# Two instructions of each chunk's preparation, the scan on VectorE and the logarithm on ScalarE, kept at their written place among the dense steps

## The chip, the cores and the metric

The kernel runs on one core of a Trainium2 chip. The metric is the device time of one launch in microseconds (us). The core's engines each work through a queue of their own, in order: TensorE (PE; its weight loads are listed as PEld), VectorE (DVE), ScalarE (ACT), GpSimd (POOL) and SyncE (SP), which here starts nearly all transfers. An instruction waits at the head of its queue until what it reads is written and what it overwrites is no longer needed, and all that stands behind it on that engine waits too.

## What is computed

```python
# batch 4, heads 8, sequence 768, head size 48
for t in range(S):                       # attention with a decaying state
    state = alpha[:, :, t, :, None] * state + einsum('bhd,bhe->bhde', k[:, :, t], v[:, :, t])
    y[:, :, t] = einsum('bhd,bhde->bhe', q[:, :, t], state)
x = y.transpose(0, 2, 1, 3).reshape(3072, 384)
h = x @ w_in                             # 384 -> 2048
x = (maximum(h, 0) + moe_alpha * minimum(h, 0)) @ w_out          # 2048 -> 384
a, b = x @ w1, x @ w2                    # 384 -> 1024
out = (a * b @ w3) @ w_out2              # 1024 -> 1024 -> 384
```

All of it is float32.

## The kernel before

The sequence of each batch is cut into chunks of 128 positions (`CH`): 24 chunks in all (`NSTEP`), numbered n = 0 to 23, and chunk n ends a batch where n leaves 5 when divided by 6. The tokens are also cut into six tiles T of 512 (`TA`), four chunks to a tile. A matrix product of float32 accuracy is made of three products of shorter parts (high by high, high by low, low by high), so that one product of a weight block takes nine matmuls of 512 columns.

For each chunk, `prep(n)` makes from the decays a running product P (`scan`, a scan on VectorE, line 221), then on ScalarE its logarithm (`Ln`, line 235) and the exponential of minus that (`Exp`, line 236), which gives 1/P in `r`; VectorE makes q times P (`qt`, line 228), k times r (`kn`, line 237), P times r (line 238) and from both the corrected `kn` (line 239), which I call the last kn. `scores(n)` is 32 small matmuls of `kn` and `qt` (tile `scp`, recorded at line 244), masked on VectorE (`sc`, line 279). `kT(n)` turns `kn` over on TensorE. `chunk(n)` forms the update of the state (`uy`), the output of the chunk (`yp`, `uy`), and then, at its end, `scores(n + 1)`.

The dense steps of the first layer are `G1(T, f)`, nine matmuls into the tile `h` and then the chain u (ScalarE, line 419), g (VectorE, 421), high part of gs (ScalarE, 426), low part of gs (VectorE, 427); and `G2(T, f)`, nine matmuls of gs into three accumulators (lines 435, 436, 438), two steps later. When a tile is through, its three accumulators are copied out on ScalarE (tile `x1e`, line 73).

The attention of tile T is woven into the dense steps of tile T - 1: `attn_units` lists pieces of work (`chunk(n)`, `kT(n + 1)`, `prep(n + 2)`, in that order), and `attend()` hands out the next piece after every G1 and every G2, evenly over the steps. So `prep(n + 1)` is written about one dense step ahead of `chunk(n)`, whose end needs its `kn`.

What is written is not yet the order of the engines. On SyncE the order is as written. On the other engines a scheduler orders the instructions when the kernel is built: by its own estimate of times it takes, as an engine comes free, an instruction that it holds to be ready. `tc.keep_in_program_order(ins)` binds one instruction behind the one that is written ahead of it on its engine. In the kernel before, u and g of G1 are bound so from T = 2 on, the matmuls of the attention among themselves, and the scan only in the opening. The buffers of P (`albuf`) are two, that of `r` is one.

Of the kernel before, what the change touches and what calls it, by code (L numbers as in the profile page):

```python
# [15 lines left out]
AF = mybir.ActivationFunctionType  # L16
# [16 lines left out]
SPT = TA // CH  # L33
# [31 lines left out]
def fused_kernel(ctx, tc, qk, al, vv, wf, ws, m_alpha, ident, maskn, out):  # L65
    nc = tc.nc
    act, dve, pool, pe, sp = nc.scalar, nc.vector, nc.gpsimd, nc.tensor, nc.sync

    def f32(ap):
        return ap.bitcast(F32)  # L70
# [144 lines left out]
    def prep(n, last=False):  # L215
        if n >= NSTEP:
            return
        t = st.pop(("qk", n))
        P = albuf[n % 2]
        flatP = P.rearrange("p a t -> p (a t)")  # L220
        scan = dve.tensor_tensor_scan(out=flatP, data0=flatP, data1=scan1.rearrange("p a t -> p (a t)"),  # L221
                                      initial=0.0, op0=ALU.mult, op1=ALU.max)
        if last:
            tc.keep_in_program_order(scan)
        pool.memset(P[:, :, 0:1], 0.0)
        Pv = P[:, :, 1:]
        qt = ap2.tile([128, NP, CH], F32, tag="qt", name="qt")
        dve.tensor_tensor(out=qt, in0=t[:, 0], in1=Pv, op=ALU.mult)
        r = ap2.tile([128, NP, CH], F32, tag="r", name="r", bufs=1)
        kn = ap2.tile([128, NP, CH], F32, tag="kn", name="kn")  # L230
        pend = ap2.tile([128, NP, 1], F32, tag="pend", name="pend")
        pool.tensor_copy(out=pend, in_=P[:, :, CH:])
        st["pend", n], st["qt", n], st["kn", n] = pend, qt, kn

        act.activation(out=r, in_=Pv, func=AF.Ln)
        act.activation(out=r, in_=r, func=AF.Exp, scale=-1.0)
        dve.tensor_tensor(out=kn, in0=t[:, 1], in1=r, op=ALU.mult)
        dve.tensor_tensor(out=r, in0=Pv, in1=r, op=ALU.mult)
        dve.scalar_tensor_tensor(out=kn, in0=r, scalar=2.0, in1=kn, op0=ALU.subtract, op1=ALU.mult)
# [143 lines left out]
    def attn_units(T):  # L383
        w = T % 2
        n0 = T * SPT
        u = []
        if T == 2:
            u += [lambda: prep(n0), lambda: load(n0 + 2)]
        if T <= 2:
            u += [lambda: (untie(), scores(n0, w), kT(n0, w)), lambda: prep(n0 + 1)]  # L390
        for n in range(n0, n0 + SPT):
            ahead = T > 1 or n < n0 + SPT - 1
            u += [lambda n=n, ahead=ahead: (ahead and load(n + 3), chunk(n, w, ahead)),
                  lambda n=n, ahead=ahead: ahead and kT(n + 1, w)]
            if T > 1 or n < n0 + SPT - 2:
                u += [lambda n=n: prep(n + 2)]
            if n == n0 + 2:
                u += [lambda: xsplit(T, 0, 2)]
        return u
# [4 lines left out]
    def mm3(ps, pairs, first, last):  # L404
        n = len(pairs)
        for i, (w, x) in enumerate(pairs):
            pe.matmul(ps, w, x, start=first and i == 0, stop=last and i == n - 1)  # L407
# [4 lines left out]
    def G1(T, f):  # L412
        x, w = xt[T], r_in[f]
        ps = pab.tile([128, TA], F32, tag="h", name="h")
        mm3(ps, [(w[:, i, k], x[:, 0, k]) for k in range(KD) for i in range(2)]
            + [(w[:, 0, k], x[:, 1, k]) for k in range(KD)], True, True)
        sg, sa = sgn[:, f:f + 1], salpha[:, f:f + 1]
        u = gp.tile([128, TA], F32, tag="m", name="u", bufs=1)
        both = [act.activation(out=u, in_=ps, func=AF.Identity, scale=sg)]  # L419
        gt = gp.tile([128, TA], F32, tag="g", name="g")  # L420
        both += [dve.scalar_tensor_tensor(out=gt, in0=ps, scalar=sa, in1=u, op0=ALU.mult, op1=ALU.max)]  # L421
        if T > 1:
            for ins in both:
                tc.keep_in_program_order(ins)
        s = g_t[T, f] = gp.tile([128, 2, TA], F32R, tag="gs", name="gs", bufs=3)
        act.activation(out=s[:, 0], in_=gt, func=AF.Identity, scale=sg)  # L426
        dve.scalar_tensor_tensor(out=s[:, 1], in0=gt, scalar=sg, in1=f32(s[:, 0]), op0=ALU.mult, op1=ALU.subtract)  # L427
# [17 lines left out]
    with tc.manual_schedule(engines={mybir.EngineType.SP}):  # L445
# [65 lines left out]
        for g in range(NG + LAG):  # L511
            T, f = seq[g] if g < NG else (NTA, 0)
# [50 lines left out]
            if g < NG:  # L563
                G1(T, f)
                attend()
# [87 lines left out]
        for q in range(NTA * NJ):  # L653
            T, j = divmod(q, NJ)
# [19 lines left out]
    with tc.If(bad > 0):  # L674
        with tc.tile_pool(name="fa", bufs=1) as fa:
# [5 lines left out]
            with tc.For_i(0, B, 1) as b:  # L681
                dve.memset(S_, 0.0)
                with tc.For_i(0, NC_B, 1) as c:
# [7 lines left out]
                    for g in range(CH // TG):  # L691
                        yt = fa.tile([2, TG, NP, D], F32, name="yt")
                        for i in range(TG):
# [10 lines left out]
                            for hh in range(2):  # L704
                                r = slice(64 * hh, 64 * hh + 64)
# [11 lines left out]
                        for k, to, a, e, n_, g_ in whole + [piece + (KD,) for piece in PIECES]:  # L717
                            hh, pr = g_ // 2, 2 * (g_ % 2) + a
                            sp.dma_start(out=dst[:, :, :, k, to:to + n_].rearrange("b c t e -> (b c) t e"),
                                         in_=yt[hh:hh + 1, :, pr, e:e + n_])  # L720

        with tc.tile_pool(name="fb", bufs=1) as fb:
# [6 lines left out]
            for f in range(NF):  # L729
                for o, dst in enumerate((wi[:, f].rearrange("p k f -> p (k f)"), wo[:, f])):  # L730
                    t = fb.tile([128, DM, 2], I32, name="rw")
                    sp.dma_start(out=t.bitcast(I16).rearrange("p n c -> p (n c)")[:, :4 * DM - 1],
                                 in_=wf[f, :, o].bitcast(I16)[:, 1:])
# [88 lines left out]
```

## Time and profile before

| | |
|---|---|
| three runs | 844.17, 847.43, 847.84 us (median 847.43) |
| the profiled execution | 846.02 us, of which the span from first to last instruction is 844.2 us |
| PE | 824.3 us busy (98% of the span) in 5160 matmuls |
| DVE | 458.3 us busy (54%) |
| ACT | 355.3 us busy (42%) |
| POOL | 10.3 us busy (1%) |
| granted TensorE clock, mean | 0.998 of full speed |

Busy time is what an engine's instructions took; the rest of the span it waited. A matmul of 512 columns is listed with 0.39 us, but the next one starts 0.23 us after it, so the starts say how fast TensorE goes. An idle time is listed with the instruction that ended it and with what that instruction had waited for. The three figures behind each wait are the sum, the number of times, and the longest.

### The profile page before, as it was taken

What the parts mean: (1) busy time and instruction counts of PE and PEld (TensorE: products, weight loads), DVE (VectorE), ACT (ScalarE), POOL (GpSimd) and SP (SyncE); (2) the same over time, 40 slices, a digit from 0 to 9 for tenths busy, and PEclk for the clock granted to TensorE, in tenths of its full rate; (3) what the DMA queues carried; (4) which work ended last, traced back from release to release, by engine and by line L of the source; (5) the groups of instructions that cost most, each with busy time, mean ns of one, the idle gap of its engine ahead of it and who ended that gap; (6) DMA issues with size and microseconds to landing.
All of it is one profiled execution on the core that took longest, in us unless ns stands there. A gap on an engine that the chain in (4) does not pass through costs nothing.

```text
span 844.2 us, 12696 instructions
## 1 busy us (share of the span) xinstructions
PE 824.3 (98%) x5160; PEld 673.1 (80%) x5160; DVE 458.3 (54%) x643; ACT 355.3 (42%) x562; POOL 10.3 (1%) x53
## 2 busy tenths in 40 slices
PE   8989999999999999999999999999999999999996
PEld 4567888888887788878888889988888888888885
DVE  7799966774766576765345634652434425322221
ACT  4568764534544554554335634522223232222222
POOL 0000000000000000000000000000000000000000
PEclk9999999999999999999999999999999999999999
DMA  8647555330774377354104207320402203010101
GB/s 314 212 168 245 197 176 183 118 110 10 225 236 146 119 231 256 131 165 168 48 3 159 78 1 255 119 75 1 150 0 75 75 31 119 1 38 0 38 1 41
DMA packets 49106, 99.60 MB, mean 118 GB/s; under 512 B 4880, under 2 KB 25488, under 8 KB 49040
## 3 DMA queue, kind: packets, MB, share of 16 engines
q1 hardware_dynamic: 48800, 98.62, 34.6%
q8 instruction: 42, 0.69, 0.3%
q14 instruction: 24, 0.20, 0.1%
q10 hardware_dynamic: 240, 0.10, 0.0%
HBM read 75.63 MB, written 18.35 MB: 111 GB/s over the span
## 4 chain that ended last, share of the span: by engine, by line
PE 83%; DMA 2%; DVE 1%; ACT 1%; issue 0%; SPq 0%; DVEq 0%; ACTq 0%
PE ab L407 23%; PE h L407 20%; PE acc L407 12%; PE acc L435 6%; PE acc L438 6%; PE acc L436 6%; PE w L407 4%; PE uy L244 3%; DMA al<-in_al_dram 2%; PE scp L244 2%; PE yp L244 1%; PE kTp L263 1%; DVE al L221 0%; DVE y L149 0%; ACT u L419 0%
## 5 line engine op out<-in xcount | busy, mean ns | idle before, releaser
L407 PE MATMUL h<-x,w 128*128 128x512 f32 x864 | 214.3, 392 | 3.2 <-ACT w L73 1.4
L407 PE MATMUL ab<-x,w 128*128 128x512 f32 x864 | 203.6, 389 | 0.0
L407 PEld LDWEIGHTS h<-x,w 128*128 128x128 f32 x864 | 160.9, 188 | 39.8 <-DVE g L421 2.6
L407 PEld LDWEIGHTS ab<-x,w 128*128 128x128 f32 x864 | 162.1, 188 | 33.6
L435 PE MATMUL acc<-gs,w 128*128 128x512 f32 x288 | 114.7, 398 | 0.0
L614 DVE TENSOR_TENSOR c<-ab,a 128x512 f32<-128x512 f32 x48 | 33.1, 690 | 147.3 <-PE ab L407 147.3
L436 PE MATMUL acc<-gs,w 128*128 128x512 f32 x288 | 112.3, 390 | 0.0
L421 DVE SCALAR_TENSOR_TENSOR g<-h,salpha,u 128x512 f32<-128x512 f32 x96 | 71.8, 748 | 69.2 <-ACT u L419 69.1
L407 PE MATMUL acc<-cs,w 128*128 128x512 f32 x432 | 105.8, 389 | 0.0
L426 ACT ACTIVATE gs<-g,sgn 128x512 fp32r<-128x512 f32 x96 | 69.3, 722 | 75.5 <-DVE g L421 75.4
L419 ACT ACTIVATE u<-h,sgn 128x512 f32<-128x512 f32 x96 | 65.4, 681 | 82.5 <-PE h L407 82.4
L427 DVE SCALAR_TENSOR_TENSOR gs<-g,sgn,gs 128x512 fp32r<-128x512 f32 x96 | 71.9, 749 | 42.7 <-ACT gs L426 42.6
L407 PEld LDWEIGHTS acc<-cs,w 128*128 128x128 f32 x432 | 81.0, 188 | 17.2 <-DVE cs L617 0.4
L438 PE MATMUL acc<-gs,w 128*128 128x512 f32 x288 | 80.9, 389 | 0.0
L73 ACT ACTIVATE a<-ab 128x512 f32<-128x512 f32 x48 | 28.7, 597 | 111.9 <-PE ab L407 111.9
L73 ACT ACTIVATE cs<-c 128x512 fp32r<-128x512 f32 x48 | 30.2, 630 | 91.5 <-DVE c L614 91.5
L435 PEld LDWEIGHTS acc<-gs,w 128*128 128x128 f32 x288 | 54.1, 188 | 12.6 <-issue 1.2
L438 PEld LDWEIGHTS acc<-gs,w 128*128 128x128 f32 x288 | 54.1, 188 | 11.5
L436 PEld LDWEIGHTS acc<-gs,w 128*128 128x128 f32 x288 | 54.1, 188 | 10.5
L617 DVE TENSOR_TENSOR cs<-c,cs 128x512 fp32r<-128x512 f32 x48 | 33.2, 691 | 30.8 <-ACT cs L73 30.8
L142 ACT ACTIVATE top<-raw 128x768 f16<-128x768 bf16 (+1 forms) x39 | 41.8, 1071 | 16.9 <-DVE y L149 12.0
L221 DVE TENSOR_TENSOR_SCAN al<-al,scan 128x516 f32<-128x516 f32 x24 | 29.4, 1230 | 25.2 <-DMA al<-in_al_dram 25.2
(73 smaller groups left out, 673.8 us busy)
## 6 DMA issues: line engine op xcount, KB each, us to landing
raw<-in_ws_dram SPq DMA_DIRECT2D x22, 767.8 KB, 5.2
qk<-in_qk_dram SPq DMA_DIRECT2D x24, 512.0 KB, 5.9
raw<-in_wf_dram SPq DMA_DIRECT2D x16, 767.8 KB, 5.9
ws_d<-y SPq DMA_DIRECT2D x22, 384.0 KB, 2.6
al<-in_al_dram SPq DMA_DIRECT2D x24, 256.0 KB, 4.9
v<-in_vv_dram SPq DMA_DIRECT2D x24, 256.0 KB, 5.9
alx<-in_al_dram SPq DMA_DIRECT2D x8, 768.0 KB, 4.6
x_d<-x1e SPq DMA_DIRECT2D x18, 256.0 KB, 4.3
```

The source lines that it names most:

```text
L73: act.activation(out=out, in_=in_, func=AF.Copy)
L142: ins = act.activation(out=z[:, :n].bitcast(F16).rearrange("p (n c) -> p n c", c=2)[:, :, 1], in_=t.bitcast(BF16)[:, :, 2], func=AF.Copy)
L244: ins = pe.matmul(*a, **k)
L407: pe.matmul(ps, w, x, start=first and i == 0, stop=last and i == n - 1)
L419: both = [act.activation(out=u, in_=ps, func=AF.Identity, scale=sg)]
L421: both += [dve.scalar_tensor_tensor(out=gt, in0=ps, scalar=sa, in1=u, op0=ALU.mult, op1=ALU.max)]
L426: act.activation(out=s[:, 0], in_=gt, func=AF.Identity, scale=sg)
L427: dve.scalar_tensor_tensor(out=s[:, 1], in0=gt, scalar=sg, in1=f32(s[:, 0]), op0=ALU.mult, op1=ALU.subtract)
L435: pe.matmul(acc[T][m], r_out[f][:, 0, c], s[:, 0], start=f == 0, stop=False)
L436: pe.matmul(acc[T][m], r_out[f][:, 1, c], s[:, 0], start=False, stop=False)
L438: pe.matmul(acc[T][m], r_out[f][:, 0, c], s[:, 1], start=False, stop=f == NF - 1)
L617: dve.tensor_tensor(out=s[:, 1], in0=c, in1=f32(s[:, 0]), op=ALU.subtract)
```

## The change

Three bindings. The scan of `prep(n)` is kept in program order not only in the opening but also for n > 8, that is from chunk 9 on. The logarithm is kept in program order for the same chunks. And u and g of G1 are kept in program order from T = 1 on, where it was from T = 2 on. Nothing is computed otherwise, and no instruction is added or removed. (Behind line 235 the line numbers of the changed kernel are two higher.)

```diff
@@ prep(n, last=False)
         scan = dve.tensor_tensor_scan(out=flatP, data0=flatP, data1=scan1.rearrange("p a t -> p (a t)"),
                                       initial=0.0, op0=ALU.mult, op1=ALU.max)
-        if last:
+        if last or n > 2 * SPT:
             tc.keep_in_program_order(scan)
...
-        act.activation(out=r, in_=Pv, func=AF.Ln)
+        ln = act.activation(out=r, in_=Pv, func=AF.Ln)
+        if n > 2 * SPT:
+            tc.keep_in_program_order(ln)
         act.activation(out=r, in_=r, func=AF.Exp, scale=-1.0)
@@ G1(T, f)
-        if T > 1:
+        if T > 0:
             for ins in both:
                 tc.keep_in_program_order(ins)
```

How the engines' orders move is shown at three places. The first is VectorE around chunk 8, where the numbers behind a name tell the buffers apart: g_1559 and gs_1561 belong to one dense step, kn_1569 and al1_110 to chunk 9, kn_1700 and al0_109 to chunk 10, r_1828 to chunk 11. Before:

```order
L427 SCALAR_TENSOR_TENSOR gs_1506<-g_1504,sgn_78,gs_1506 128x512
L279 TENSOR_TENSOR sc_1529<-scp_1510,msk_76 128x512
L237 TENSOR_TENSOR kn_1700<-qk_1486,r_1699 128x512
L221 SCALAR_TENSOR_TENSOR al1_110<-al1_110,scan1_111 128x516
L238 TENSOR_TENSOR r_1699<-al0_109,r_1699 128x512
L239 SCALAR_TENSOR_TENSOR kn_1700<-r_1699,kn_1700 128x512
L421 SCALAR_TENSOR_TENSOR g_1559<-h_1547,salpha_79,u_1557 128x512
L427 SCALAR_TENSOR_TENSOR gs_1561<-g_1559,sgn_78,gs_1561 128x512
```

And now:

```order
L423 SCALAR_TENSOR_TENSOR g_1559<-h_1547,salpha_79,u_1557 128x512
L429 SCALAR_TENSOR_TENSOR gs_1561<-g_1559,sgn_78,gs_1561 128x512
L221 SCALAR_TENSOR_TENSOR al1_110<-al1_110,scan1_111 128x516
L228 TENSOR_TENSOR qt_1566<-qk_1011,al1_110 128x512
L239 TENSOR_TENSOR kn_1569<-qk_1011,r_1568 128x512
L304 TENSOR_TENSOR sst1_113<-sst0_112,yT_1618 128x256
L240 TENSOR_TENSOR r_1568<-al1_110,r_1568 128x512
L306 TENSOR_TENSOR sst1_113<-sst1_113,pend_1464 128x256
L241 SCALAR_TENSOR_TENSOR kn_1569<-r_1568,kn_1569 128x512
```

Before, at this place VectorE already prepares chunk 10 and scans chunk 11, and chunk 9 has long been prepared; now the scan of chunk 9 stands behind gs_1561, and its last kn closes the row. From chunk 9 on each scan stands in this way behind the gs written ahead of it.

The second place is TensorE at the same chunk: the matmuls that close `chunk(8)`, and the scores of chunk 9 (`scp`). Before:

```order
L244 MATMUL yp<-qt,sst_112 64x128
L244 MATMUL scp<-qt,kn 64x128 x16
L407 MATMUL h<-x,w_86 128x512 x9
L263 MATMUL kTp<-idn,kn 128x128 x4
L435 MATMUL acc_1429<-gs,w_84 128x512
L436 MATMUL acc_1429<-gs,w_84 128x512
```

And now:

```order
L246 MATMUL yp<-qt,sst_112 64x128
L409 MATMUL h<-x,w_86 128x512 x9
L437 MATMUL acc_1429<-gs,w_84 128x512
L438 MATMUL acc_1429<-gs,w_84 128x512
L437 MATMUL acc_1430<-gs,w_84 128x512
L438 MATMUL acc_1430<-gs,w_84 128x512
L246 MATMUL scp<-qt,kn 64x128 x16
L265 MATMUL kTp<-idn,kn 128x128 x4
```

The scores have gone back behind nine matmuls of G1 and four of G2. (A row counts 16 of the 32 score matmuls, since those of the two halves are listed together.) The same happens to the scores of ten chunks: 9 and 10 go back by G1 and four of G2, 11 by G1 and five, 12 by nine of G2 and one of the G1 behind it, 14 and 22 by four of G2, 15 by seven, 18 and 19 by eight, 23 by three. The scores of 13, 16, 17, 20 and 21 keep their place.

The third place is ScalarE at the end of a tile, where the accumulators acc_2339 to acc_2341 are copied out. Before:

```order
L426 ACTIVATE gs<-g,sgn 128x512
L235 ACTIVATE r<-al_110 128x512
L236 ACTIVATE r<-r 128x512
L73 ACTIVATE x1e<-acc_2339 128x512
L73 ACTIVATE x1e<-acc_2340 128x512
```

And now:

```order
L428 ACTIVATE gs<-g,sgn 128x512
L73 ACTIVATE x1e<-acc_2339 128x512
L73 ACTIVATE x1e<-acc_2340 128x512
L73 ACTIVATE x1e<-acc_2341 128x512
L73 ACTIVATE yT<-uy 128x4x128
```

The logarithm and the exponential (of chunk 19) stood ahead of the copies; now they come after them. The order on SyncE is the same in both kernels; on GpSimd small clears and copies of P change places by one.

## Rows read from the trace of the kernel before

**Rows 1.** Busy time of each engine in stretches of 20 us: bounds and length of the stretch, busy us of PE, PEld, DVE, ACT and POOL with the number of instructions, granted TensorE clock, share of the DMA engines, GB/s.

```profile
240.00:260.00 20.00, 18.99 (x152) 15.35 (x151) 11.96 (x18) 8.86 (x14) 0.29 (x2) 1.00 0.50 171
...
280.00:300.00 20.00, 18.59 (x151) 14.97 (x152) 12.45 (x19) 10.54 (x17) 0.30 (x2) 1.00 0.52 164
300.00:320.00 20.00, 20.00 (x196) 16.45 (x193) 13.79 (x20) 10.73 (x18) 0.29 (x2) 1.00 0.72 243
...
360.00:380.00 20.00, 18.98 (x153) 15.40 (x151) 13.00 (x19) 10.72 (x17) 0.29 (x2) 1.00 0.55 177
```

**Rows 2.** Who waited for whom, PE alone: us in total, times, longest.

```profile
PE uy L244 <- ACT x1e L73: 2.4, 2, 1.4
...
PE h L407 <- DVE g L421: 1.2, 2, 1.0
```

**Rows 3.** Instructions in order of time, all engines, 255 to 260 us: start, length in us, engine, line, operation, in brackets the idle time of the engine before it and what ended that.

```profile
255.76 1.23 DVE L221 TENSOR_TENSOR_SCAN al<-al,scan 128x516 f32<-128x516 f32 x1 [4.55 <-DMA al<-in_al_dram]
...
257.02 0.63 ACT L235 ACTIVATE r<-al 128x512 f32<-128x512 f32 x1 [5.06 <-DVE al L221]
...
257.69 0.63 ACT L236 ACTIVATE r<-r 128x512 f32<-128x512 f32 x1
...
258.23 0.67 ACT L419 ACTIVATE u<-h,sgn 128x512 f32<-128x512 f32 x1
258.93 0.75 DVE L421 SCALAR_TENSOR_TENSOR g<-h,salpha,u 128x512 f32<-128x512 f32 x1 [1.30 <-ACT u L419]
...
259.74 2.35 PE L407 MATMUL h<-x,w 128*128 128x512 f32 x9 [1.01 <-DVE g L421]
```

**Rows 4.** The same view at the ends of two tiles, 285 to 289 us and 368 to 369 us.

```profile
285.79 1.23 DVE L221 TENSOR_TENSOR_SCAN al<-al,scan 128x516 f32<-128x516 f32 x1 [1.27 <-DMA al<-in_al_dram]
...
288.25 1.55 ACT L73 ACTIVATE x1e<-acc 128x512 f32<-128x512 f32 x3
...
288.88 0.69 PE L244 MATMUL uy<-v,kT 128*64 128x64 f32 x16 [1.41 <-ACT x1e L73]
...
368.76 0.69 PE L244 MATMUL uy<-v,kT 128*64 128x64 f32 x16 [1.02 <-ACT x1e L73]
```

**Rows 5.** The same view of one dense step with nothing between, 276 to 282 us: G1's matmuls, the first of the G2 behind them, and the chain u, g, high and low part of gs.

```profile
276.66 2.20 PE L407 MATMUL h<-x,w 128*128 128x512 f32 x9
...
278.70 0.39 PE L435 MATMUL acc<-gs,w 128*128 128x512 f32 x1
...
278.96 0.69 ACT L419 ACTIVATE u<-h,sgn 128x512 f32<-128x512 f32 x1 [0.88 <-PE h L407]
...
279.68 0.75 DVE L421 SCALAR_TENSOR_TENSOR g<-h,salpha,u 128x512 f32<-128x512 f32 x1 [0.61 <-ACT u L419]
...
280.47 0.72 ACT L426 ACTIVATE gs<-g,sgn 128x512 fp32r<-128x512 f32 x1 [0.82 <-DVE g L421]
...
281.23 0.75 DVE L427 SCALAR_TENSOR_TENSOR gs<-g,sgn,gs 128x512 fp32r<-128x512 f32 x1 [0.79 <-ACT gs L426]
```

**Rows 6.** The same view, VectorE alone, for the distance from one start to the next: a state update (sst) and the op behind it; a gs and the op behind it; the P times r of a chunk and the last kn, which reads it.

```profile
52.16 0.42 DVE L304 TENSOR_TENSOR sst<-sst,pend 128x256 f32<-128x256 f32 x1
52.49 0.95 DVE L154 TENSOR_TENSOR w<-y,w 128x768 fp32r<-128x768 f32 x1
...
156.30 0.75 DVE L427 SCALAR_TENSOR_TENSOR gs<-g,sgn,gs 128x512 fp32r<-128x512 f32 x1 [0.79 <-ACT gs L426]
156.96 0.68 DVE L228 TENSOR_TENSOR qt<-qk,al 128x512 f32<-128x512 f32 x1
...
160.82 0.68 DVE L238 TENSOR_TENSOR r<-al,r 128x512 f32<-128x512 f32 x1
161.54 0.69 DVE L239 SCALAR_TENSOR_TENSOR kn<-r,kn 128x512 f32<-128x512 f32 x1
```

**Rows 7.** The same view, PE alone, at `chunk(8)`: the first matmul behind the G1 whose gs the scan now follows, the scores of chunk 9, the G1 and the kT behind them.

```profile
139.37 0.39 PE L435 MATMUL acc<-gs,w 128*128 128x512 f32 x1
...
143.48 1.05 PE L244 MATMUL scp<-qt,kn 48*64 48x128 f32 x32
144.46 2.34 PE L407 MATMUL h<-x,w 128*128 128x512 f32 x9
146.64 0.60 PE L263 MATMUL kTp<-idn,kn 128*128 128x128 f32 x4
```

**Rows 8.** The same at `chunk(11)`, `chunk(13)`, `chunk(17)` and `chunk(18)`: in each pair the first matmul behind that G1, and the scores of chunks 12, 14, 18 and 19.

```profile
174.34 0.39 PE L435 MATMUL acc<-gs,w 128*128 128x512 f32 x1
...
180.02 1.06 PE L244 MATMUL scp<-qt,kn 48*64 48x128 f32 x32
...
213.84 0.39 PE L435 MATMUL acc<-gs,w 128*128 128x512 f32 x1
...
219.54 1.05 PE L244 MATMUL scp<-qt,kn 48*64 48x128 f32 x32
...
296.08 0.39 PE L435 MATMUL acc<-gs,w 128*128 128x512 f32 x1
...
301.31 1.06 PE L244 MATMUL scp<-qt,kn 48*64 48x128 f32 x32
...
311.05 0.39 PE L435 MATMUL acc<-gs,w 128*128 128x512 f32 x1
...
316.72 1.10 PE L244 MATMUL scp<-qt,kn 48*64 48x128 f32 x32
```

## What I predict

> **What bounds the kernel now.** I read the stretches of 20 us first. TensorE is the bound: in most stretches it is busy from end to end, as in 300 to 320, and only three stretches in the middle miss something, 1.01 us from 240 to 260, 1.41 from 280 to 300 and 1.02 from 360 to 380 [rows 1]. VectorE and ScalarE are busy for half to three quarters of the same stretches, so their amount of work is no limit there; what counts is when a result comes. Next the list of waits, where the three gaps have names: the state update at the end of a tile waits for `x1e` (2.4 us in two waits), and G1 waits for g (1.2 in two, the longest 1.0) [rows 2].
>
> Then the order of time at the gaps. At 255.76 VectorE starts a scan after idling 4.55 us for the decays, and ScalarE has stood 5.06 us at its head with the logarithm that reads this scan. u, ready long before, comes after the exponential at 258.23, g at 258.93, and TensorE, which needs the buffer of `h` that g reads, starts at 259.74, 1.01 us late [rows 3]. At 285.79 the same scan waits for the decays again, and behind its logarithm and exponential stand the copies `x1e`: the first runs at 288.25 and frees the accumulator for `uy` at 288.88, 1.41 us late. The end of the next tile is the same at 368.76, with 1.02 us [rows 4]. So all three gaps come from preparing a chunk as soon as its decays land, in front of work that TensorE needs first.
>
> **The change part by part.** Nothing is added: 15 scans and 15 logarithms move, and their exponentials, products and `qt` with them.
>
> What it removes. In the new order the logarithm of chunk 19 stands behind `x1e`, and each scan behind a gs that is written ahead of it, about two chunks after its decays were asked for. The three gaps lose their cause: 1.01 + 1.41 + 1.02 = 3.4 us gained. In the opening, VectorE gets rid of the early preparation of chunk 9; TensorE idles there for reasons outside the moved work, so I count nothing.
>
> What it adds. The scores of a chunk now need a last kn that is made in the same breath. Ten groups of scores have been moved back by 3 to 13 large matmuls to leave time for it. Whether that is enough I work out from starts. Time 0 is the start of the first matmul behind the G1 whose gs the scan follows.
>
> The chain, from a dense step with nothing in between: u at 0.26 (278.96 - 278.70), low gs at 2.53 (281.23 - 278.70) [rows 5]. The op behind a gs starts 0.66 later [rows 6], so the scan starts at 3.19 and ends at 4.42; the logarithm comes 0.03 after it (257.02 - 255.76 - 1.23), at 4.45, the exponential 0.67 later, at 5.12, and ends at 5.75 [rows 3]. A handover between engines costs 0.04 (g ends at 280.43, ScalarE's gs starts at 280.47) [rows 5]: k times r at 5.79. The two products behind it each need the one before, 0.72 from start to start [rows 6]: 6.51 and 7.23. The last kn is through at 7.92, and the scores can start at **7.96**.
>
> Where other work stands between, it adds. For chunks 9 to 11 two state updates stand in the chain, each 0.33 [rows 6], and each opens it once: 5.79 + 0.60 + 0.33 = 6.72 for P times r, 7.65 for the last kn, scores at 8.4. (0.60 is a 0.68 op less the overlap of 0.09 that the gs pair shows.) For chunk 11 a split of x also stands behind the scan, where VectorE waits for the exponential anyway. For chunk 12 a u stands ahead of the exponential, 0.54 after the logarithm's place in line (258.23 - 257.69) [rows 3], a g ahead of k times r and a low gs ahead of the last kn: g from about 5.7, k times r at 6.36, P times r at 7.08, the gs at 7.68, the last kn at 8.34, scores at 9.1. For 19 one state update: 8.2. For 14, 18, 22 and 23 nothing counts: 7.96.
>
> TensorE gets to the scores as follows. At chunk 9 they started at 143.48 - 139.37 = 4.11 before; now G1 (146.64 - 144.46 = 2.18) [rows 7] and four matmuls of 0.227 (2.04 for nine, 278.70 - 276.66) [rows 5] stand ahead: 4.11 + 2.18 + 0.91 = 7.20. Late by 8.4 - 7.2 = 1.2 us. Chunk 10 has the same order and 1.2; 11, with five, 1.0. The others, from their own starts before [rows 8]: chunk 12, 180.02 - 174.34 + 10 x 0.227 = 7.95, late by 1.1; 14, 219.54 - 213.84 + 0.91 = 6.61, late by 1.35; 18, 301.31 - 296.08 + 8 x 0.227 = 7.05, late by 0.9; 19, 316.72 - 311.05 + 1.82 = 7.49, late by 0.7. Chunk 22 is ordered as 14 (1.35). For chunks 15 and 23 a G2 and a G1 lie between time 0 and the chunk, where at chunk 9 it is a G2 alone: 4.11 + 2.04 = 6.15, plus seven or three matmuls; 23 is at 6.83 and late by 1.1. For 15, 7.74 is set against a chain with a split of x and a state update in it; I take the 1.2 of chunk 9. Sum: 1.2 + 1.2 + 1.0 + 1.1 + 1.35 + 1.2 + 0.9 + 0.7 + 1.35 + 1.1 = **11.1 us**. The scores of 16 and 20 stand two dense steps behind their scan (about 10 us), and those of 13, 17 and 21 more: nothing there.
>
> Behind the waiting scores on TensorE stand kT and the rest of a G2, and behind those everything; TensorE has no slack later in which it could make this up [rows 1], so each wait counts in full.
>
> Bounds. Below: no wait at all, if the chain is 1 us shorter at each place. Above: one more dense op of 0.75 [rows 5] ahead at each of the ten, 7.5 us more, 18.6. I take the sum, since each link has a row from this kernel.
>
> The u and g of T = 1 stand where they stood but for a place or two among conversions; those, and the small clears on GpSimd, I cost at nothing: TensorE does not wait for them before, and if u slipped by one op there it would cost at most 0.7 us once. SyncE's order stays, but the load of decays for chunk n + 3 waits for P of n + 1, now read to the end at about 7.2 on the clock above instead of much earlier. Behind it stand the loads of q, k, v and of the raw weights. The decays are needed two chunks later; I count nothing, and below what it costs otherwise.
>
> One rule speaks for a longer chain. Rows first: two dependent products of 0.68 us start 0.72 apart, and an op behind a gs of 0.75 starts 0.66 after it, before its end [rows 6]. The Trainium skill, "VectorE: DVE Perf Modes", section "The DRAIN you can't avoid", has each VectorE op followed by a flush of its own length less 266 ns. As an estimate by that page, the gs and the two products would add 0.5 + 0.4 + 0.4 us to each chain and some 13 us to the sum. The trace does not agree, and I leave it out.
>
> **The forecast.** The profiled execution took 846.02 us; 846.0 + 11.1 - 3.4 = **853.7 us**, 0.9% more. The three runs lie from 844.2 to 847.8, with the median 1.4 above the profiled one, so I make no correction. About 0.5% (4.2 us) is what a measurement here can tell from no change: the edges are 843.2 and 851.7.
>
> **The rivals.**
> *The gaps go and nothing comes* (the other side). The moved scores may stand far enough back: it decides at a last kn done about 1.1 us earlier than I have it, at each place. For it: three to thirteen large matmuls now stand ahead of them. Against it: every link of the chain has a row. 846.0 - 3.4 = 842.6 us.
> *Half.* The chain is shorter, or TensorE slower at the turns from small to large matmuls, by some 0.5 us at each place: 5 to 6 of waits, 848 us; the span of this case is 844.6 to 849.6.
> *SyncE or the clock.* If raw weights came late because SyncE stands at the decays, ScalarE would wait with their conversion in front of u, and each of ten chunks could lose what a late u costs now, 1.0 us [rows 3]: 864 us. Against it: decays and weights are asked for more than a chunk ahead. Or TensorE's clock could fall after the new waits: a G1 at the lower level (1.2 GHz) is 4.08 for 2.04, ten times 2.0: 874 us. Against that, the granted clock is 1.00 in the stretch that holds the 1.41 us gap [rows 1]. The Trainium skill, "TensorE: Matmul & The Clock Gate", section on the HAM clock gate, tells of the halved clock after idleness; after gaps of this length no row here shows it.
> *The change does nothing.* The orders rule that out.
>
> **How the numbers follow.** My case, 0.7 to 1.6 us at each of the ten places (net 850 to 858.6): 0.62. Half: 0.17. No waits: 0.12. Worse, above 858.6: 0.09. The range takes my case and Half, which is 8 in 10: 844.6 to 859. Faster by over 0.5%: 0.11 (the case without waits). Within: 0.28 (Half, and the low end of mine). Slower: 0.61.
>
> **What would show it.** The gaps at the ends of the tiles and before 260 gone, `x1e` early; new waits of `scp` for the last kn, about ten, of 0.7 to 1.4 us, 11 in sum; logarithms that no longer wait for decays. I am wrong if those waits are few or under 0.3 us, if the ends of tiles still wait, or if TensorE waits for ScalarE behind a late raw weight.

## The result, and the profile after

The changed kernel takes 856.11 us (median of four runs, 855.36 to 857.19), the kernel before 847.24 in the same comparison: a ratio of 1.0101, with a 95% interval of 1.0079 to 1.0122. It is slower by 1%, where 853.7 had been forecast. The profiled execution took 856.12 us, its span 854.3. In the experiments below, one execution of e2 took 1182.03 us at a mean granted clock of 0.655, and e2's ratio leaves it out.

First the page of the changed kernel: busy time by engine, and the shares of the chain of work that ended last. The third line is that chain in the kernel before.

```profile
PE 827.9 (97%) x5160; PEld 672.4 (79%) x5160; DVE 461.8 (54%) x643; ACT 357.2 (42%) x562; POOL 16.2 (2%) x53
...
PE 77%; DVE 10%; ACT 5%; DMA 3%; issue 3%; SPq 2%; ACTq 0%; DVEq 0%
...
PE 83%; DMA 2%; DVE 1%; ACT 1%; issue 0%; SPq 0%; DVEq 0%; ACTq 0%
```

The busy times are nearly those of before, but VectorE and ScalarE now hold 15% of the chain that ends last, where they held 2%. What TensorE waits for, the list of waits of PE says (total, times, longest); `x1e` and g, which stood in it before [rows 2], are gone. This is its first line; from 140 us on the list has no other:

```profile
PE scp L246 <- DVE kn L241: 11.6, 13, 1.4
```

Three of the 13 lie in the first 140 us. The other ten are the displaced scores. In order of time, PE alone, with the idle time ahead of each in brackets (the scores of 9, 10, 11, 12, 14, 15, 18, 19, 22 and 23):

```profile
148.84 1.10 PE L246 MATMUL scp<-qt,kn 48*64 48x128 f32 x32 [1.03 <-DVE kn L241]
...
162.08 1.10 PE L246 MATMUL scp<-qt,kn 48*64 48x128 f32 x32 [1.03 <-DVE kn L241]
...
175.29 1.10 PE L246 MATMUL scp<-qt,kn 48*64 48x128 f32 x32 [0.80 <-DVE kn L241]
...
188.60 1.10 PE L246 MATMUL scp<-qt,kn 48*64 48x128 f32 x32 [0.82 <-DVE kn L241]
...
228.28 1.10 PE L246 MATMUL scp<-qt,kn 48*64 48x128 f32 x32 [1.07 <-DVE kn L241]
...
246.31 1.10 PE L246 MATMUL scp<-qt,kn 48*64 48x128 f32 x32 [1.00 <-DVE kn L241]
...
311.26 1.10 PE L246 MATMUL scp<-qt,kn 48*64 48x128 f32 x32 [0.79 <-DVE kn L241]
...
327.52 1.10 PE L246 MATMUL scp<-qt,kn 48*64 48x128 f32 x32 [0.51 <-DVE kn L241]
...
392.51 1.10 PE L246 MATMUL scp<-qt,kn 48*64 48x128 f32 x32 [1.07 <-DVE kn L241]
...
409.47 0.78 PE L246 MATMUL scp<-qt,kn 48*64 48x128 f32 x20 [0.85 <-DVE kn L241]
```

The brackets sum to 8.97 us. They count from the end of the matmul ahead, which is listed with 0.39, while the next could start 0.23 after its start; so each group is late by 0.16 more, and the ten together by 10.6 us.

The stretches show both sides (columns as in [rows 1]): from 280 to 300 and from 360 to 380 nothing is missing any more, and from 300 to 320, which was full, 0.79 us is.

```profile
280.00:300.00 20.00, 20.00 (x156) 16.48 (x155) 11.34 (x17) 11.65 (x18) 0.52 (x1) 1.00 0.50 172
300.00:320.00 20.00, 19.21 (x138) 15.27 (x138) 14.38 (x20) 9.96 (x16) 0.65 (x2) 1.00 0.68 214
360.00:380.00 20.00, 20.00 (x156) 16.50 (x155) 11.22 (x16) 10.99 (x18) 0.65 (x2) 1.00 0.49 171
```

The sharpest measure is the distance from the first matmul of one chunk (`uy`) to that of the next. It contains the same matmuls in both kernels and nothing of the opening. Of before and of the changed kernel, chunks 8 and 9:

```profile
141.50 0.69 PE L244 MATMUL uy<-v,kT 128*64 128x64 f32 x16
...
153.31 0.69 PE L244 MATMUL uy<-v,kT 128*64 128x64 f32 x16
```

```profile
142.48 0.69 PE L246 MATMUL uy<-v,kT 128*64 128x64 f32 x16
...
155.72 0.69 PE L246 MATMUL uy<-v,kT 128*64 128x64 f32 x16
```

That is 11.81 before and 13.24 after, 1.43 more. All distances in this way, as differences from the kernel before (us; the experiments' columns are used further below):

| from chunk to chunk | changed | prep early (e3) | scores late (e4) | Ln only (e6) | Ln of 19, 23 (e8) | and prep(19) early (e9) |
|---|---|---|---|---|---|---|
| 8 to 9 | +1.43 | +1.53 | +1.41 | +0.62 | 0.00 | +0.01 |
| 9 to 10 | +1.39 | +1.29 | +1.40 | +0.63 | 0.00 | -0.01 |
| 10 to 11 | +1.28 | -0.19 | +1.29 | +0.90 | 0.00 | +0.01 |
| 11 to 12 | +1.29 | +0.30 | +0.31 | +0.68 | 0.00 | 0.00 |
| 12 to 13 | 0.00 | -0.01 | +0.13 | -0.01 | 0.00 | -0.01 |
| 13 to 14 | +1.52 | +0.63 | +0.53 | +0.37 | 0.00 | +0.01 |
| 14 to 15 | +1.45 | 0.00 | +0.30 | +1.74 | 0.00 | -0.01 |
| 15 to 16 | -2.38 | -2.79 | -2.10 | -2.79 | -2.70 | -2.76 |
| 16 to 17 | -0.03 | -0.02 | +0.40 | -0.02 | -0.03 | -0.03 |
| 17 to 18 | +1.25 | +1.19 | +0.76 | +0.75 | 0.00 | 0.00 |
| 18 to 19 | +0.81 | -0.01 | +0.14 | +0.26 | +1.65 | +0.63 |
| 19 to 20 | -0.94 | -1.32 | -0.65 | -1.32 | -1.32 | -1.21 |
| 20 to 21 | -0.01 | -0.01 | +0.30 | -0.01 | -0.01 | -0.01 |
| 21 to 22 | +1.51 | +0.64 | +0.53 | +0.36 | 0.00 | 0.00 |
| 22 to 23 | +1.30 | -0.01 | +0.42 | -0.01 | 0.00 | 0.00 |
| sum, 8 to 23 | +9.87 | +1.22 | +5.17 | +2.15 | -2.41 | -3.38 |

In the changed kernel the ten displaced places cost 13.2 us, and the distances that hold the tile ends and the gap before 260 (15 to 16 and 19 to 20) give 3.3 back. The opening up to chunk 8 was 0.98 longer in this execution (142.48 against 141.50) and the rest behind chunk 23 some 0.7 shorter, which makes up the 10.1 by which the spans differ.

### The profile page after: what moved, and what is told of

Its sections match the earlier page's. It is cut to its first block, busy times and chain, and to the rows that moved or that the text cites. A ratio compares the mean times of both kernels' runs of the same rounds, so it can differ in the third digit from the quotient of the medians.

```text
span 854.3 us, 12708 instructions
## 1 busy us (share of the span) xinstructions
PE 827.9 (97%) x5160; PEld 672.4 (79%) x5160; DVE 461.8 (54%) x643; ACT 357.2 (42%) x562; POOL 16.2 (2%) x53
## 4 chain that ended last, share of the span: by engine, by line
PE 77%; DVE 10%; ACT 5%; DMA 3%; issue 3%; SPq 2%; ACTq 0%; DVEq 0%
PE ab L409 23%; PE h L409 17%; PE acc L409 11%; PE acc L440 6%; PE acc L437 6%; PE acc L438 6%; PE w L409 4%; DVE al L221 2%; PE scp L246 2%; DMA raw<-in_wf_dram 2%; DVE g L423 1%; DMA x<-yT 1%; ACT u L421 1%; ACT gs L428 1%; PE uy L246 1%
## 5 line engine op out<-in xcount | busy, mean ns | idle before, releaser
L409 PEld LDWEIGHTS acc<-cs,w 128*128 128x128 f32 x432 | 81.0, 188 | 17.2 <-DVE cs L619 0.4
L438 PEld LDWEIGHTS acc<-gs,w 128*128 128x128 f32 x288 | 54.1, 188 | 10.6 <-issue 0.3
L149 DVE SCALAR_TENSOR_TENSOR y<-raw,top 128x768 int32<-128x768 int32 (+1 forms) x39 | 36.8, 944 | 2.6 <-ACT top L142 2.6
```

The costliest lines, as they stand in the source:

```text
L149: return dve.scalar_tensor_tensor(out=y, in0=t[:, :, 0], scalar=13, in1=z[:, :n], op0=ALU.logical_shift_right, op1=ALU.bitwise_or)
L438: pe.matmul(acc[T][m], r_out[f][:, 1, c], s[:, 0], start=False, stop=False)
```

## The experiments

Theory A, from the prediction: the bound chain is late at the displaced scores; the gaps that vanish give some of it back. Theory B: another of the three bindings does it. Theory C: the loss isn't lateness, but what else the new order does to TensorE. Each experiment was run beside the kernel before on the same chip (847.1 to 847.7 us there).

**The three bindings apart.** First u and g of G1 back to what they were, then the reverse, then the scan alone, then the logarithm alone.

```
e1:  -        if T > 0:                          (G1; scan and Ln stay bound)
     +        if T > 1:
e2:  only  if T > 0:  in G1; scan and Ln as before
e5:  only  if last or n > 2 * SPT: keep_in_program_order(scan)
e6:  only  if n > 2 * SPT: keep_in_program_order(ln)
```

> The changed kernel with one of its three bindings undone: u and g of G1 are bound from T = 2 on again, as before; scan and logarithm stay bound. TensorE's order is that of the changed kernel. Theory A (the ten groups of scores that wait for the last kn cost about 13 us, the three gaps that vanish give 3.4 back, and the 1 us that the opening lost up to chunk 8 is variation between executions): 855.5 to 856.5, the ten waits unchanged at 0.5 to 1.1 each. Theory B (the binding of u and g in T = 1 costs the opening its 1 us): about 855.0, and the first chunk 8 matmul starts near 141.5 us and not near 142.5.

Measured: 856.82 us, ratio 1.0114 (1.0071 to 1.0157). The median is 0.3 us above theory A's range, with executions from 855.09 to 859.67. Chunk 8 starts at 142.85 us, and the scores of 9 wait 1.03 us. The binding of u and g has no part in it.

> The kernel before with only the binding of u and g of G1 from T = 1 on; scan and logarithm as before. Theory A: 847 within 1 us, with the three gaps of 1.01, 1.41 and 1.02 us and none of the ten waits. Theory B (this binding costs the opening 1 us): about 848.2, and chunk 8 starts near 142.5 us.

Measured: 846.76 us, ratio 0.9989 (0.9974 to 1.0004), with the waits for `x1e` in place (2.5 us, two times). The gap before 260, though, was not there. The two longest waits for g and for `x1e` in this run:

```profile
PE uy L244 <- ACT x1e L73: 2.5, 2, 1.8
...
PE h L407 <- DVE g L421: 0.6, 2, 0.4
```

So the length of the first of the three gaps, 1.0 us, belongs to one execution; in this one the wait for g was at most 0.4, and one for `x1e` 0.4 longer than in [rows 4]. Between chunks 15 and 16 TensorE, VectorE and ScalarE run the same order as in the kernel before. Chunk 15 starts 2.90 us later (256.33 against 253.43) and the decays land only 1.74 later, so VectorE idles 2.54 us for them where it idled 4.55 [rows 3], and the distance from 15 to 16 is 0.80 shorter:

```profile
257.50 1.23 DVE L221 TENSOR_TENSOR_SCAN al<-al,scan 128x516 f32<-128x516 f32 x1 [2.54 <-DMA al<-in_al_dram]
```

> Of the three bindings only that of the scan. TensorE's order is that of the changed kernel, and the logarithm of 19 and 23 comes after the three copies of x1e there too, since it can't go ahead of its scan. Theory A (the bound scan alone makes the chain late and alone takes the gaps away): 855 to 857, the ten waits as in the changed kernel. Theory B (the bound logarithm is needed for the loss): nearer to 850.

Measured: 857.21 us, ratio 1.0114 (1.0098 to 1.0129), all fifteen distances those of the changed kernel to 0.03 us. The binding of the scan alone does all that the change does.

> Of the three bindings only that of the logarithm. In TensorE's order the scores of 9, 10 and 11 go back by the nine matmuls of G1, those of 12 and 18 by one, those of 19 by four; the other 18 of the chunks keep their place of before. The chain is shorter by the scan, which stays early (1.23 us). Theory A (every displaced group is late by what the estimate of the order misses, about 1 us, whatever the chain's length): six waits of 0.6 to 1.1 us, 6 places at 1.2 to 1.4 by distance = 7 to 8, gaps gone 3.4: 850 to 852. Rival (a shorter chain is on time): waits under 0.3, 843 to 846.

Measured: 850.26 us, ratio 1.0034 (1.0023 to 1.0044). The time is as theory A has it, the places aren't. The waits at 9 to 12 are near the rival's, 0.24 to 0.43 where the changed kernel has 0.80 to 1.03; and the scores of 15, which kept their place, wait longest:

```profile
148.74 1.10 PE L246 MATMUL scp<-qt,kn 48*64 48x128 f32 x32 [0.26 <-DVE kn L241]
...
242.87 1.10 PE L246 MATMUL scp<-qt,kn 48*64 48x128 f32 x32 [1.52 <-DVE kn L241]
```

So "about 1 us, whatever the chain's length" is false. How late a group is depends on the chain and on the place of each.

**Earlier, or later.** If lateness is all, the wait must go when the chain is written earlier, or the scores later.

```
e3:  +            if T > 1:
     +                u += [lambda n=n: prep(n + 2)]      # directly behind chunk(n)
                  u += [lambda: ahead and kT(n + 1, w)]
     -            if T > 1 or ...:
     +            if T <= 1 and ...:
                      u += [lambda n=n: prep(n + 2)]      # where it was
e4:  -   chunk(n, w, ahead)                 # ends in scores(n + 1)
     +   chunk(n, w, ahead and T < 2)
     ...
     +   (untie(), scores(n + 1, w))        # T >= 2: ahead of kT(n + 1), in its piece; its first matmul unbound
```

> All three bindings, but from T = 2 on the preparation of the chunk after next is written directly behind chunk(n), ahead of kT(n + 1), so that the bound scan stands one piece of work earlier among the dense steps. Theory A (the loss is the lateness of the bound chain, about 1.2 us at each of ten groups of scores): one piece earlier is worth 2 us or more at each place, the waits for the last kn vanish and the three gaps stay away: 843 to 846, faster than both kernels. Theory C (the loss is not the lateness but what the bindings take from the scheduler elsewhere, or the split of G2 by small matmuls): 852 to 856.

Measured: 847.77 us, ratio 1.0017 (0.9997 to 1.0037): 8.3 us of the loss are gone, as theory A has it, but the time is 1.8 us above theory A's range and the kernel no faster than before. The scores wait no more except at 9, whose preparation is not moved by this edit, and at 10 (0.29). What is left shows in the table: 1.5 us at 9; 1.3 at 10, where the state update of chunk 10 also waits 0.48 for the copy of `kT`; and 0.6 to 1.2 us at 13, 17 and 21, where the order splits the group of `uy` and `yp` by matmuls of G2 and the output waits some 0.2 for g. Two rows of PE of this run, at chunk 13:

```profile
222.87 0.50 PE L440 MATMUL acc<-gs,w 128*128 128x512 f32 x1
...
225.31 1.05 PE L246 MATMUL scp<-qt,kn 48*64 48x128 f32 x32
```

The first stands in the middle of the chunk's output, behind which its scores then come at 225.31, 3.50 us after the chunk's start at 221.81; before it was 1.98 (219.54 [rows 8] less 217.56).

> All three bindings, but scores(n + 1) of the chunks from T = 2 on are written one piece later, with kT(n + 1) instead of at the end of chunk(n). In TensorE's order the scores of 9, 10 and 11 stay where the changed kernel has them, those of 12 and later go back by five matmuls or more. Theory A: the waits of 9, 10 and 11 stay (1.03, 1.03 and 0.80 us; by distance between chunk starts 4.1 us together), the other seven vanish (9 us by those distances), the gaps stay away: about 847 to 849, with chunk 12 starting near 213.0 us as in the changed kernel. Theory C (the loss comes from elsewhere): 853 to 856.

Measured: 853.53 us, ratio 1.0066 (1.0044 to 1.0087). The seven waits vanished, those of 9, 10 and 11 stayed at 1.04, 1.04 and 0.81. The total is theory C's, 4.5 us above theory A's range. The seven distances did not fall by 9.1 us to nothing: 3.0 stayed, and the five distances without a displaced group lost 1.4 against the changed kernel. Here is one of the seven, now without any wait, at chunk 14:

```profile
246.70 2.20 PE L409 MATMUL h<-x,w 128*128 128x512 f32 x9
248.84 1.10 PE L246 MATMUL scp<-qt,kn 48*64 48x128 f32 x32
249.87 0.65 PE L265 MATMUL kTp<-idn,kn 128*128 128x128 f32 x4
250.28 0.47 PE L437 MATMUL acc<-gs,w 128*128 128x512 f32 x1
```

Nine matmuls of G1 take 2.04 from start to start [rows 5], here the scores come after 2.14; the scores take 1.03 instead of the 0.98 of [rows 7], and G2 comes 0.41 after kT instead of 0.35 (146.99 less 146.64 in the kernel before). The first large matmul behind the output comes 0.20 after it, where the scores followed after 0.09. Together that is 0.32, and the distance from 14 to 15 is 0.30 longer than before. A group of scores that stands alone between large matmuls costs some 0.3 us by its turns, waited for or not; at 12 to 13 and 18 to 19, where in the kernel before too the scores followed after 0.20, it is 0.13 and 0.14. Theory C is right for a part. At 13 to 14, 17 to 18 and 21 to 22 (0.53, 0.76 and 0.53) something more is lost, and what it is stays open. The rest of the miss is the opening: chunk 8 starts at 145.42 in the profiled execution, and the granted clock was 0.91 in its first 20 us and 0.93 from 80 to 100.

**A longer chain.** One VectorE instruction more, or the scan twice.

```
e7:   +  dve.scalar_tensor_tensor(out=kn, in0=kn, scalar=1.0, in1=kn, op0=ALU.mult, op1=ALU.max)
e11:  +  if n > 2 * SPT: keep_in_program_order(dve.tensor_tensor_scan(out=qt, data0=P, data1=scan1, ...))
         scan = dve.tensor_tensor_scan(out=P, data0=P, data1=scan1, ...)
```

> The changed kernel with one more instruction on VectorE at the end of each chunk's chain, which writes kn again with the same values (kn = max(1.0 x kn, kn), of the form of the last kn: 0.75 us, the next starts 0.68 after it). TensorE's order answers: the scores of the ten chunks go back by another 3 to 5 matmuls (0.7 to 1.1 us), and those of 17 and 21, which did not move so far, go behind one matmul of G2 that also splits the output group. Theory A (the order follows its own estimate of the chain, which is short by a fixed amount, so that a longer chain moves the scores and leaves the lateness): waits for kn at the same places, each 0.8 to 1.3 us as before or less, 856 to 859. Rival (the lateness grows with the chain, 0.68 a place): waits of 1.5 to 1.8, 862 to 864.

Measured: 863.45 us, ratio 1.0182 (1.0166 to 1.0197). The total is the rival's, and would have misled: by place it is theory A that holds. At chunk 9 the wait is 1.07 where it was 1.03, and from chunk 8 to chunk 9 it is 13.28 where it was 13.24:

```profile
155.70 1.10 PE L247 MATMUL scp<-qt,kn 48*64 48x128 f32 x32 [1.07 <-DVE kn L242]
```

The order moved the scores by three matmuls (0.68 us), the chip lengthened the chain by 0.72 (the instruction took 0.69, not 0.75). The total was lost elsewhere: the instruction also stands in the chains of the opening, and chunk 8 starts 6.1 us later. In the first 140 us the waits of scores for kn are 8.7 us, against 2.5 in the changed kernel; the granted clock was 0.91 from 0 to 20 and from 40 to 60 us, and how the 6.1 divide between the two is open.

```profile
PE scp L247 <- DVE kn L242: 8.7, 4, 3.7
```

> The changed kernel with the scan of chunks 9 to 23 made twice, first into the buffer of qt (overwritten later), both bound; the results are the same. The chain grows by the 1.15 us at which a VectorE instruction follows a scan; TensorE's order puts the scores of 9 and 10 four matmuls (0.91 us) further back, those of 17 and 21 behind one matmul of G2 that splits the output group. Theory A (the wait of a group of scores is the chain as the chip makes it, less the place that the order gives it): the wait of the scores of 9 is 1.03 + 1.15 - 0.91 = 1.27, chunk 8 to chunk 9 13.5 us, the whole 860 to 862. Rival (the wait is a fixed price of the turn to small matmuls, or grows by the whole scan): 1.03, or 2.2 us.

Measured: 867.81 us, ratio 1.0244 (1.0225 to 1.0263). The wait at 9 is 1.65, neither of the rival's two figures, but not 1.27 either:

```profile
150.50 1.10 PE L251 MATMUL scp<-qt,kn 48*64 48x128 f32 x32 [1.65 <-DVE kn L246]
```

ScalarE shows why (start, length, line, idle before):

```profile
146.19 0.63 ACT L240 ACTIVATE r<-al 128x512 f32<-128x512 f32 x1 [3.22 <-DVE al L227]
146.73 0.58 ACT L73 ACTIVATE yT<-uy 128x512 f32<-128x512 f32 x1
147.21 0.62 ACT L243 ACTIVATE r<-r 128x512 f32<-128x512 f32 x1
```

The second scan added 1.25 (143.68 to 144.93), not 1.15, and a copy `yT` stands between logarithm and exponential. Both chains set against the same instant (time 0 of the prediction), the last kn comes 1.52 later than in the changed kernel; 1.03 + 1.52 - 0.91 = 1.64. The formula of theory A holds at 9, my chain in it was short. The total is 6 us above theory A's range: against the changed kernel the ten displaced places lose 5.6 us more, and the two distances with the tile ends, which gave 3.3 back, lose 0.3.

**Only what closes the gaps.** Of the 15 logarithms two stood ahead of `x1e` [rows 4]. The others needn't be bound at all, and no scan.

```
e8:   +  if n in (19, 23): tc.keep_in_program_order(ln)
e9:   the same, and for n = 17 prep(n + 2) directly behind chunk(n)
e10:  +  if n == 23: tc.keep_in_program_order(ln)
```

> The kernel before with one binding: the logarithm of chunks 19 and 23 alone is kept in program order. TensorE's order is that of the kernel before; on ScalarE the logarithm and the exponential of 19 and of 23 come after the three copies of x1e, those of 20 follow. Theory A (the gaps of 1.41 and 1.02 us at the ends of two tiles are the logarithm and exponential ahead of the copies, and nothing else is moved): those two gaps gone, no new wait, 2.4 less than before: 844 to 845.5, faster than both kernels. Rival (the copies come no earlier, or the later logarithm is waited for by the scores of 19, 20 or 23): 847 or more, with a wait of scores for kn.

Measured: 845.31 us, ratio 0.9972 (0.9962 to 0.9983). The time is as theory A has it, the reason only half. The copies run as soon as the accumulators are done, 1.34 us after ScalarE was free; and the scores of 19 do wait:

```profile
287.39 1.58 ACT L73 ACTIVATE x1e<-acc 128x512 f32<-128x512 f32 x3 [1.34 <-PE acc L440]
```

```profile
317.65 1.10 PE L246 MATMUL scp<-qt,kn 48*64 48x128 f32 x32 [1.58 <-DVE kn L241]
```

Against the profiled execution of before the two tile ends give 2.70 and 1.32, and chunk 18 to 19 takes 1.65 back. The 2.70 contains the gap before 260, which that execution had; against e2 and e10, whose order from 15 to 16 is that of before and which didn't have it (0.80 and 0.76 shorter there), it is 1.9.

> The kernel before with the logarithm of 19 and 23 bound, and prep(19) written one piece earlier, directly behind chunk(17). In the run with those two bindings alone the gaps at the tile ends were gone, but the scores of 19 waited 1.58 us for kn, and chunk 18 to chunk 19 took 21.19 us where it had been 19.54. Theory A (a binding is harmless when the chain behind it is written a dense step earlier): that wait is gone, the distance is 19.5 again, 1.65 less than that run: 843.3 to 844.3. Rival (the earlier chain makes something else late, the update of the state or the chain u, g, gs of the same step): 845 to 847, with a wait between 299 and 320 us.

Measured: 844.46 us, ratio 0.9957 (0.9940 to 0.9973), 3.1 us less than before: the lowest median here, and faster than both. It misses theory A's range by 0.2. The intervals of e8 and e9 overlap, so by the total the two can't be told apart; by distances e9 is 1.0 us ahead. The last kn of 19 starts at 314.98, the scores at 317.85 without a wait for it. Of the 1.65 us, 1.0 came back; the rest is what the rival named, a wait of the chunk's output for g, behind which the earlier products now stand on VectorE:

```profile
317.26 0.66 PE L246 MATMUL yp<-sc,v 128*64 128x128 f32 x8 [0.42 <-DVE g L427]
```

> The kernel before with the logarithm of chunk 23 alone bound; TensorE's order is that of the kernel before. Theory A: only the second tile end (1.02 us of gap; the distance of chunk 19 to chunk 20 fell by 1.32 in the run with 19 and 23 bound) is mended and nothing waits instead: 1.0 to 1.3 less than before. Rival (the gap is made up for later): as before.

Measured: 846.79 us, ratio 0.9983 (0.9972 to 0.9995), 0.8 less, where theory A had 1.0 to 1.3. The second `x1e` wait is gone, the first stays (1.63); a wait of 0.65 for g at 343 took part of the gain.

## Why the prediction was right, and where it was short

**Right, and shown.** The place, the cause and the size of the waits. Set to time 0 (the first matmul of the G2 at 140.35), the chain at chunk 9 runs in the changed kernel as follows, VectorE and ScalarE:

```profile
142.87 0.75 DVE L429 SCALAR_TENSOR_TENSOR gs<-g,sgn,gs 128x512 fp32r<-128x512 f32 x1 [0.79 <-ACT gs L428]
143.54 1.22 DVE L221 TENSOR_TENSOR_SCAN al<-al,scan 128x516 f32<-128x516 f32 x1
...
146.13 0.69 DVE L239 TENSOR_TENSOR kn<-qk,r 128x512 f32<-128x512 f32 x1 [0.64 <-ACT r L238]
146.74 0.42 DVE L304 TENSOR_TENSOR sst<-sst,yT 128x256 f32<-128x256 f32 x1
147.07 0.68 DVE L240 TENSOR_TENSOR r<-al,r 128x512 f32<-128x512 f32 x1
147.68 0.41 DVE L306 TENSOR_TENSOR sst<-sst,pend 128x256 f32<-128x256 f32 x1
148.01 0.68 DVE L241 SCALAR_TENSOR_TENSOR kn<-r,kn 128x512 f32<-128x512 f32 x1
```

```profile
144.80 0.63 ACT L235 ACTIVATE r<-al 128x512 f32<-128x512 f32 x1 [1.96 <-DVE al L221]
145.47 0.63 ACT L238 ACTIVATE r<-r 128x512 f32<-128x512 f32 x1
```

Scan 3.19, logarithm 4.45, exponential 5.12, k times r 5.78, P times r 6.72, last kn 7.66, scores 8.49: the forecast had 3.19, 4.45, 5.12, 5.79, 6.72, 7.65 and 8.4. The handovers between VectorE and ScalarE took the 0.03 and 0.04 of the forecast; the last step, from the end of the last kn (148.69) to the scores, took 0.15 where the forecast had 0.04. The lateness of the ten places (bracket plus 0.16), against the forecast, and what the distances of the table hold beyond it:

| scores of | 9 | 10 | 11 | 12 | 14 | 15 | 18 | 19 | 22 | 23 | sum |
|---|---|---|---|---|---|---|---|---|---|---|---|
| late, forecast | 1.2 | 1.2 | 1.0 | 1.1 | 1.35 | 1.2 | 0.9 | 0.7 | 1.35 | 1.1 | 11.1 |
| late, measured | 1.19 | 1.19 | 0.96 | 0.98 | 1.23 | 1.16 | 0.95 | 0.67 | 1.23 | 1.01 | 10.6 |
| distance, beyond it | 0.24 | 0.20 | 0.32 | 0.31 | 0.29 | 0.29 | 0.30 | 0.14 | 0.28 | 0.29 | 2.7 |

That each wait counts in full was right too: every distance is longer by at least its wait. The Trainium skill ("VectorE: DVE Perf Modes", section "The DRAIN you can't avoid") tells of a flush of an op's length less 266 ns behind each VectorE op, and that a next op which is not held starts earlier. By its figures the flush would have added an estimated 1.3 us to this chain. The trace has no room for it: the scan starts 0.67 after a gs of 0.75, the state update 0.61 after k times r of 0.69. Leaving it out was right.

**Right in size, by luck for a part.** The gains were forecast at 3.4 us and came to 3.3. But the 1.0 us of the gap before 260 belongs to the one execution that the forecast was made from; in e2 and e10 the engines run that place in the same order and are 0.8 us faster there. That the logarithm ahead of `x1e` is worth most of the gain, e8 shows. And the sum of the waits was 0.5 too high, which hides a part of the term that was left out.

**Short.** The step that fell short is "What it adds": it counted the waits and nothing else. Each displaced group of scores also pays for standing alone between large matmuls, the last row of the table, 2.7 us at ten places. At chunk 9 G1 starts 0.20 after the last matmul of the output, where before the scores followed after 0.09 (143.39 to 143.48). Two rows of PE of the changed kernel:

```profile
144.37 0.27 PE L246 MATMUL yp<-qt,sst 64*64 64x128 f32 x1
144.57 2.33 PE L409 MATMUL h<-x,w 128*128 128x512 f32 x9
```

To these 0.11 come 0.06 (the scores take 1.04 for 0.98) and 0.06 (G2 comes 0.41 after kT for 0.35), 0.23 in all; 1.19 + 0.23 is the 1.43 of the table to 0.01. At 19, where in the kernel before too the scores followed the output after 0.20, the least is left, 0.14. The turn could have been read from the kernel before: there G1 starts 0.20 after the last score of chunk 9. The prediction named "TensorE slower at the turns" in its rival Half as a reason for a shorter wait; the wait was as long as forecast and the turns came on top. One reading of [rows 1] is to be set right, though nothing hangs on it: ScalarE is busy for 44 to 54% of those stretches, not for half to three quarters.

**Not the change.** The forecast was made from an execution of 846.02, and the kernel before has its median at 847.1 over 22 runs. Chunk 8 starts at 141.50 in that execution and at 142.48 in the changed kernel, but with the scan free also at 144.41 (e2), 143.51 (e8) and 144.48 (e10). In these three the granted clock was 0.91 in the first 20 us. From chunk 1 to chunk 8, with the clock at 1.00 from 20 to 140 us in all of them, the scan left free takes 123.3 to 125.2 us (before, e2, e8, e10) and the scan bound 124.2 to 124.6 (changed, e1, e3, e5, e11). So the 0.98 us of the opening lie inside the variation between executions, and no effect of the moved preparation of chunk 9 shows in them.

**The rivals.** No waits: refuted by ten of them. Half: refuted, the ten places are late by 10.6 us in sum where it had 5 to 6. SyncE and the clock: the granted clock is 1.00 in each stretch shown above, and from 140 us on TensorE's list names no raw weight and no ScalarE. Nothing: refuted.

**Open.** Why the estimate of the order is short. e7 and e11 show that the order follows the chain's length (by 0.68 where the chip took 0.72, by 0.91 where it took 1.52); with the scan free (e6) the scores stand four matmuls earlier (0.91), the last kn comes some 1.7 earlier, and 0.8 of the lateness goes. So most of the miss lies in the bound scan and what it waits for. Which part of it, the wait behind the gs or the scan's own length, these runs don't separate.

## What to carry to other kernels

Binding an instruction to its written place moves its whole chain, and with it whoever needs the chain's end; work the chain out start by start from the rows and set it against the place where the order now puts the consumer. Bind only the instructions that the waits name: two logarithms instead of 15 scans and 15 logarithms turned 1% slower into 0.3% faster (0.4% with one chain written earlier, which the intervals don't tell apart). Compare distances between the same two matmuls, not totals alone: e7's total spoke for the wrong theory, and its distances for the right one.

## What was not expected of the hardware

A turn between small and large matmuls costs TensorE without any wait: in the changed kernel 0.23 us for the scores of chunk 9, which stood behind other small ones and now stand behind large ones; 0.14 to 0.32 at the ten places. It is not a matter of large and small alone: inside the output, from the last matmul of `128*64` to the first of `64*64`, both kernels show 0.20 as well.

The granted clock in the opening differs between executions. It was 1.00 in each stretch of the changed kernel's profiled execution up to 140 us. In that of e4 it was 0.91 from 0 to 20 and 0.93 from 80 to 100; a stretch's figure is a mean of the two levels, 2.4 and 1.2 GHz (columns as in [rows 1]):

```profile
0.00:20.00 20.00, 16.16 (x152) 8.98 (x154) 14.82 (x27) 7.98 (x12) 1.69 (x11) 0.91 0.87 306
...
60.00:80.00 20.00, 17.36 (x122) 12.98 (x123) 17.00 (x24) 12.61 (x20) 0.18 (x2) 0.99 0.66 214
80.00:100.00 20.00, 20.00 (x175) 15.91 (x175) 19.26 (x27) 16.33 (x23) 0.70 (x1) 0.93 0.66 224
```

It fell after a stretch in which TensorE was busy for 17.4 of 20 us. The changed kernel was at 18.7 in that stretch, but e3 was at 17.7 and e2 at 17.2, and both kept 1.00; what decides it, these runs don't show. The 0.91 of the first 20 us stands in e2, e6, e8 and e10 too. Chunk 1 starts at 19.2 to 19.5 us in these and in e4, and at 18.2 to 18.3 in the seven executions with 1.00 there. Chunk 8 starts 2.9 us later in e4 than in the changed kernel, as much as single effects studied here; hence the distances behind chunk 8.
